# An index table moved into a loop, and three steps of the routing moved in a table of order (attention and mixture of experts, one core)

## The chip, the core and the metric

The kernel runs on one core of a Trainium2 chip. The core has a matrix engine (PE, with its weight loads PEld), a vector engine (DVE), a scalar engine (ACT), a general engine (POOL), a queue engine for transfers (SP) and 16 DMA engines. The metric is the time of one execution on the device, in microseconds (us). Before the change it was 745.78, 746.29 and 747.35 us in three runs, median 746.29.

## The reference

It computes attention over a window of 128 positions for 8 sequences of 576 tokens and 8 heads of 64, and sends every token of its output (x, 512 values) through one of 8 experts:

```python
logits = np.einsum('bsd,de->bse', x, w_gate)
local_gate = 1.0 / (1.0 + np.exp(-np.einsum('bsd,de->bse', x, w_local).squeeze(-1)))
for b in range(B):
    prev_e = -1
    for s in range(S):
        fresh_e = int(np.argmax(logits[b, s]))
        e = fresh_e if s == 0 or local_gate[b, s] < 0.5 else prev_e
        prev_e = e
        p = softmax(logits[b, s])
        h = np.maximum(x[b, s] @ w1[e], 0.0)
        out[b, s] = p[e] * (h @ w2[e])
```

The choice of a token can thus hang on that of the token before it. (The branch for prev_e below 0 is left out here; the first token is always fresh.)

## The kernel before, in words

**Attention.** The 8 batches (sequences) have 4 pairs of heads each, so there are 32 pairs. A slot of the program is one row of the table `ORDER` (lines 58 to 63, the row is the slot modulo 4), a string of atoms. Each atom names a step, and one slot holds steps of neighbouring pairs: a mark ' belongs to one pair earlier. Of a pair, `S` i computes scores (PE, tile sc), `D` adds the bias and takes the maximum (DVE), `E` the exponent (ACT), `N` divides by the sums (POOL scales nine parts in place, after a reciprocal on DVE), `U` j transposes four parts on PE (tile pt, two PSUM buffers; four matmuls, here called a turn), `C` j copies pt out (pts; ACT, but DVE for j = 0), `M` j multiplies with the values (PE, tiles xa and xb), `X` copies the weighted values out (ACT, tile xT), `T` transposes them on DVE for their storage. On each engine the instructions of this stage run in the order in which they are written down: `InOrder` (line 151) ties each to the one before it.

**Routing of a batch.** After a batch's last pair, a generator `side` is made of `tokens` (line 568) and `route` (line 589). A dot in `ORDER` advances it by one step, so the dots set where its steps stand among the attention's. The steps of `tokens`: logits of 512 tokens (PE into tile pk, lines 575 and after); the first copy of pk (ACT, to tile part); logits of the last 128; the second copy; transposes of part; a reduction on DVE to L; the same for the last tokens. Of `route`: DVE finds the freshest choice (rcb); four small matmuls bring the choices into a row (PE, pk from rcb); ACT makes a hold copy of it; DVE scans the row (hr); PE spreads it; DVE makes the one-hot oh_all; PE then counts the rank of each token within its expert (six matmuls, the first with weights utri); and more steps to the tables of own tiles. Tile pk has one PSUM buffer (line 82), so each use waits until the one before it is read. Seven batches are routed within the attention; the eighth's routing lies in the stage that follows.

**Experts.** Tokens that go to one expert are gathered in tiles of 128 rows. Each expert has a fixed number of own tiles (`OWN`, 9 in all); the rest is cut by size rank after a plan (`RANKS`, 32 tiles); and what goes beyond this plan is done in a loop at the end (line 1191), whose count `left` is read from the routing's result. A visit of the plan (`Fixed.run`) multiplies in three passes for each product (lines 953 to 955; h is the hidden layer, y the output), and at fixed places calls `Feed.tick`, which advances the generator `routing()`: the eighth batch's steps, then `rank_tables` (line 865). That one makes three tables: of ranks (`trk`), of counts, and of the tiles beyond the plan (`tfx`). A table is filled by `fill_table` (line 843): per batch, five compares on DVE (tile cw), five matmuls on PE (pk, from cw and ro_all, line 860), three additions on DVE; `indices` (line 696) turns it into addresses on DVE. In this stage instructions are written in the order of visits and ticks, with the matmuls pinned to it. The chunks of weights are loaded by SP's queue up to six ahead (wraw) and split into two parts by ACT and DVE (cut).

The scatters of results (`out<-y,sidx`) and all gathers (`kr<-xd,xidx`, `gs<-gd,ridx`) are issued by POOL.

Of the kernel before, what the change touches and what calls it, by code (L numbers as in the profile page):

```python
# [28 lines left out]
NSB = 128  # L29
# [19 lines left out]
def windows(nb):  # L49
    return [min(4 * t, nb - 4) for t in range((nb + 3) // 4)]  # L50
# [7 lines left out]
ORDER = [  # L58
# [4 lines left out]
]  # L63
DEPTH = 3
POOL_CUT = 19
# [6 lines left out]
def moe_attention(ctx, tc, qT, kT_d, vv, wg, wl, w1, w2, out):  # L72
    nc = tc.nc
# [44 lines left out]
    tfx = st.tile([P, NSB], F32, name="tfx")  # L118

    XO = 4 * KS, 4 * KS + NSB, 4 * KS + 2 * NSB  # L120
    TO = KS, KS + NTL, KS + NTL + NFX
# [4 lines left out]
    idxs = [xidx, ridx, sidx]  # L126
# [10 lines left out]
    def run(g):  # L137
        for _ in g:
            pass
# [163 lines left out]
    with ExitStack() as actx:  # L303
# [97 lines left out]
        def setup():  # L401

            yield from make_bias(2)
            yield from make_bias(3)
            whole = dict(channel_multiplier=0, allow_small_or_imprecise_dtypes=True)
            pool.memset(w32, 0.0)
            nc.sync.dma_start(w32[:, :, 0:8], wg.rearrange("(k p) e -> p k e", p=P))
            nc.sync.dma_start(w32[:, :, 8:9], wl.rearrange("(k p) e -> p k e", p=P))
            yield
            pool.memset(onesb, 1.0)  # L410
            yield
            pool.memset(msel, 1.0)
            yield
            pool.affine_select(utri, onesb, [[1, P]], ALU.is_gt, 0.0, base=0, channel_multiplier=-1)
            yield
            pool.affine_select(msel, msel, [[-32, 4]], ALU.is_ge, 0.0, base=0, channel_multiplier=1)
            yield
            pool.memset(first, 0.0)
            yield
            pool.iota(quart, [[32, 4]], base=0, **whole)  # L420
            yield
            pool.affine_select(msel, msel, [[32, 4]], ALU.is_ge, 0.0, base=31, channel_multiplier=-1)
            yield
            pool.memset(first[0:1, 0:1], 1.0)
            yield
            pool.iota(k8, [[0, NT], [-1, NE]], base=NE, **whole)
            yield
            pool.tensor_tensor(quart, quart, msel, ALU.mult)
            yield
            pool.tensor_copy(identb, ident)  # L430
            yield
            for t in HR:
                pool.memset(t, 0.0)
                yield
            pool.memset(ohs, 0.0)
            pool.memset(g32, 0.0)
            yield
            pool.iota(io16, [[0, NT], [1, 4 * KS]], base=0, **whole)
            yield
            pool.iota(rep32, [[0, 4], [1, 32]], base=0, **whole)  # L440
            yield
            pool.iota(val, [[P, NT]], base=1, channel_multiplier=1, allow_small_or_imprecise_dtypes=True)
            yield
            pool.memset(tbl, 0.0)
            yield
            pool.memset(tfx, 0.0)
            yield
            pool.memset(trk, 0.0)
            yield
            pool.memset(own, 0.0)  # L450
            for e, k in enumerate(OWN):
                pool.memset(own[:, e:e + 1], 4.0 * k)
            yield
            for r in range(NE):
                pool.memset(slots[:, 0, r:r + 1], float(sum(CAP[:r])))
                pool.memset(slots[:, 1, r:r + 1], float(CAP[r]))
                if r % 2:
                    yield
            pool.iota(io32, [[1, NFX]], base=0, **whole)
            yield  # L460
            pool.iota(io128, [[1, NSB]], base=1, **whole)
# [234 lines left out]
        def indices(t, idx, x0, c0, wins):  # L696

            xi, rw, sc = idx
            m, n = t.shape[1], len(wins)
            ti = tp.tile([P, NSB], I32, name="ti", bufs=1)[:, :m]  # L700
            bi = tp.tile([P, NSB], I32, name="bi", bufs=1)[:, :m]
            fi = tp.tile([P, 4 * NFX], F32, name="fi", bufs=1)
            dve.tensor_scalar(ti, t, -1.0, 0.0, ALU.add, ALU.max)
            dve.tensor_scalar(bi, ti, 5, None, ALU.arith_shift_right)
            yield
            dve.scalar_tensor_tensor(fi[:, :m], bi, 96.0, ti, ALU.mult, ALU.add)
            yield
            dve.tensor_scalar(xi[:, x0:x0 + m], fi[:, :m], roff[:, 0:1], None, ALU.add)
            yield
            t1 = tp.tile([P, NFX], F32, name="t1", bufs=1)[:, :n]  # L710
            z = tp.tile([P, NFX], F32, name="iz", bufs=1)[:, :n]
            fw = fi[:, :4 * n].rearrange("p (c q) -> p c q", q=4)
            lo = 0
            while lo < n:
                hi = lo + 1
                while hi < n and wins[hi] == wins[hi - 1] + 4:
                    hi += 1
                dve.tensor_tensor(fw[:, lo:hi], t[:, wins[lo]:wins[lo] + 4 * (hi - lo)].rearrange("p (c q) -> p c q", q=4),
                                  msel.unsqueeze(1).broadcast_to([P, hi - lo, 4]), ALU.mult)
                lo = hi  # L720
            dve.tensor_reduce(t1, fw, AX.X, ALU.add)
            yield
            dve.tensor_scalar(rw[:, c0:c0 + n], t1, -1.0, 0.0, ALU.add, ALU.max)
            dve.tensor_scalar(z, t1, 0.0, 16384.0, ALU.is_equal, ALU.mult)
            dve.scalar_tensor_tensor(sc[:, c0:c0 + n], t1, -1.0, z, ALU.add, ALU.add)
            yield
# [108 lines left out]
    def per_token(x, name):  # L835

        t8 = mp.tile([P, NA, NE], F32, name="ge", bufs=1)
        nc.vector.tensor_tensor(t8, oha, x.unsqueeze(1).broadcast_to([P, NA, NE]), ALU.mult)
        o = tp.tile([P, NA], F32, name=name, bufs=1)
        nc.vector.tensor_reduce(o, t8, AX.X, ALU.add)  # L840
        return o

    def fill_table(table, fc, pace):

        fo = {}

        def hot(b):
            fo[b] = tp.tile([P, NT, NSB], F16, name="cw")
            for t in range(NT):
                nc.vector.tensor_scalar(fo[b][:, t], io128, fc[:, b * NT + t:b * NT + t + 1], None, ALU.is_equal)  # L850

        hot(0)
        for b in range(NB):
            for _ in range(pace // 2):
                yield
            if b + 1 < NB:
                hot(b + 1)
            pt = ptk.tile([P, NSB], F32, name="pk")
            for t in range(NT):
                pin(nc.tensor.matmul(pt, ro_all[:, b, t], fo[b][:, t], start=t == 0, stop=t == NT - 1))  # L860
            for _ in range(pace - pace // 2):
                yield
            enter(table, pt, b)

    def rank_tables():
# [58 lines left out]
        off = small("off")  # L924
# [7 lines left out]
        nc.vector.tensor_reduce(ef, ge, AX.X, ALU.add)  # L932
        nc.vector.tensor_scalar(efx[:, 0:NFX], ef, float(NE - 1), None, ALU.min)
        yield
        b_t = per_token(off, "at_t")
        nc.vector.tensor_tensor(b_t, b_t, ka, ALU.add)
        nc.vector.scalar_tensor_tensor(b_t, b_t, 1.0, hi_t, ALU.add, ALU.mult)
        yield
        yield from fill_table(tfx, b_t, 4)
        yield from indices(tfx, idxs, XO[1], TO[1], windows(NSB))  # L940
        nc.sync.dma_start(xidx_d, xidx[:, XO[1]:])
        nc.sync.dma_start(ridx_d, ridx[:, TO[1]:])
        nc.sync.dma_start(sidx_d, sidx[:, TO[1]:])
# [153 lines left out]

    route_done, rank_done, table_done = [], [], []  # L1100

    def routing():
        yield from chain(tokens(NB - 1, last_xT), route(NB - 1))
# [85 lines left out]
    left = nc.values_load(efx[0:1, NFX:NFX + 1], min_val=0, max_val=NFX)  # L1189
    line.clear()  # L1190
    with tc.For_i(0, left, 1) as i:
        gc = mp.tile([P, 4], I32, name="gc")
        rc = mp.tile([P, 1], I32, name="rc")
        sc = mp.tile([P, 1], I32, name="sc")
        ec = mp.tile([1, 1], I32, name="ec")
        nc.sync.dma_start(gc, xidx_d.rearrange("p (c q) -> p c q", q=4)[:, bass.ds(i, 1)].rearrange("p o q -> p (o q)"))
        nc.sync.dma_start(rc, ridx_d[:, bass.ds(i, 1)])
        nc.sync.dma_start(sc, sidx_d[:, bass.ds(i, 1)])
        nc.sync.dma_start(ec, efx_d[0:1, bass.ds(i, 1)])
        ev = nc.sync.value_load(ec[0:1, 0:1], min_val=0, max_val=NE - 1)  # L1200
        v = Flex(gc, rc, sc)
        at_once(v)
        v.run(Stream([(ev, w, c) for w, c in FLEX_ORDER]), lambda: None)
        scatter(*pending.pop())
# [36 lines left out]
```

## Time and profile before

| what | us |
|---|---|
| median of three runs | 746.29 |
| the profiled execution | 746.64 |
| its span, from the first instruction to the last | 744.9 |
| PE busy | 715.9 (96%) |
| DVE busy | 504.8 (68%) |
| ACT busy | 431.4 (58%) |
| POOL busy | 403.1 (54%) |

The rows of the profile read: start, duration, engine, line, operation, the written tile, an arrow, the read tiles, the shapes; xN is a count of like instructions in a row, and [a <-b] says that the engine was idle for a us before and that b ended it. Matmuls overlap, so the distance of two starts tells what one costs. Times are us from the start of the span. In the attention stage most lines stand as L157, a helper's line; the tiles tell them apart.

### The profile page before, as it was taken

To read this page: it belongs to the slowest core of one execution; us is meant where nothing else is said; L and a number is where in the kernel's file an instruction comes from. 1 tells how busy PE (TensorE), PEld (TensorE's weight loads), DVE (VectorE), ACT (ScalarE), POOL (GpSimd) and SP (SyncE) were. 2 spreads that over 40 slices of the span, in tenths; PEclk is the share of its full clock that TensorE was granted. 3 is DMA by queue.
4 is the path that set the end of the run, shared out by engine and by line. 5 is a ranking of instruction groups with operands and counts; after the bars stand their busy time and mean duration, and the time that the engine had idled before them with its cause. 6 is when DMAs were issued, how large, how long until landed. Compare 5 with 4: busy or idle time off the path is not lost. (4 is left out here: it accounts for less than half of the span.)

```text
span 744.9 us, 15003 instructions
## 1 busy us (share of the span) xinstructions
PE 715.9 (96%) x4669; PEld 599.7 (81%) x4669; DVE 504.8 (68%) x1743; ACT 431.4 (58%) x1204; POOL 403.1 (54%) x672
## 2 busy tenths in 40 slices
PE   7999999999999998998999999999999999999996
PEld 4777777777777777886888888989989987888895
DVE  7658686776869789998667375567567556536562
ACT  7778878878877875433333254355455446434553
POOL 7664554544558586587777153744745746402121
PEclk9999999999999999999999999999999999999999
DMA  9975636555370357545455256557657656535560
GB/s 222 194 205 127 181 98 177 181 146 167 98 260 28 104 168 250 163 142 150 131 150 178 91 174 207 181 176 224 192 170 229 196 166 210 170 91 185 164 177 30
DMA packets 94724, 122.01 MB, mean 164 GB/s; under 512 B 46961, under 2 KB 65777, under 8 KB 94642
## 3 DMA queue, kind: packets, MB, share of 16 engines
q1 hardware_dynamic: 83810, 100.36, 45.2%
q0 software_dynamic: 9488, 20.22, 9.0%
q8 instruction: 37, 0.61, 0.3%
q10 hardware_dynamic: 1344, 0.46, 0.3%
q14 instruction: 45, 0.37, 0.2%
HBM read 101.29 MB, written 20.30 MB: 163 GB/s over the span
## 5 line engine op out<-in xcount | busy, mean ns | idle before, releaser
L234 DVE TENSOR_TENSOR cut<-wraw,cut 128x512 fp32r<-128x512 f32 x231 | 150.5, 687 | 51.3 <-ACT cut L232 50.1
L172 POOL DMA_INDIRECT kr<-xd,xidx x141 | 154.5, 1096 | 52.8 <-issue 40.3
L232 ACT CAST cut<-wraw 128x512 fp32r<-128x512 f32 x212 | 120.7, 618 | 56.0 <-PE y L955 55.7
L953 PE MATMUL h<-qx,cut 128*128 128x384 f32 (+6 forms) x440 | 142.7, 325 | 2.9 <-ACT qx L181 2.9
L954 PE MATMUL h<-qx,cut 128*128 128x384 f32 (+6 forms) x440 | 142.6, 324 | 0.5 <-DVE qx L182 0.5
L955 PE MATMUL h<-qx,cut 128*128 128x384 f32 (+6 forms) x440 | 142.1, 323 | 0.0
L157 POOL TENSOR_SCALAR cut<-cut,r 128x192 f32<-128x192 f32 (+2 forms) x256 | 99.6, 407 | 69.3 <-PE pt L157 41.0
L953 PE MATMUL y<-cut,hh 128*128 128x512 f32 x328 | 129.2, 394 | 1.1 <-ACT hh L998 1.1
L955 PE MATMUL y<-cut,hl 128*128 128x512 f32 x328 | 128.8, 396 | 0.5 <-DVE hl L999 0.5
L954 PE MATMUL y<-cut,hh 128*128 128x512 f32 x328 | 129.1, 393 | 0.0
L947 POOL DMA_INDIRECT out<-y,sidx x41 | 43.2, 1053 | 155.6 <-ACT y L962 120.5
L998 ACT ACTIVATE hh<-h 128x384 fp32r<-128x384 f32 (+6 forms) x104 | 47.9, 460 | 131.3 <-PE h L955 131.1
L157 PE MATMUL sc<-kr,qx 128*128 128x192 f32 (+1 forms) x576 | 110.4, 320 | 2.8 <-DVE mn L157 1.7
L157 ACT ACTIVATE cut<-scs,mn 128x192 f32<-128x192 f32 (+2 forms) x256 | 109.6, 430 | 5.5 <-DVE mn L157 3.7
L157 DVE CUSTOM_DVE_ANT_0 scs<-sc,bias 128x192 f32<-128x192 f32 (+2 forms) x288 | 86.4, 325 | 36.1 <-PE sc L157 34.1
L999 DVE SCALAR_TENSOR_TENSOR hl<-h,hh 128x384 fp32r<-128x384 f32 (+6 forms) x112 | 56.6, 505 | 71.3 <-ACT hh L998 69.4
L953 PEld LDWEIGHTS h<-qx,cut 128*128 128x128 f32 x440 | 84.0, 191 | 10.0 <-ACT qx L181 3.3
L157 PEld LDWEIGHTS sc<-kr,qx 128*128 128x128 f32 x576 | 85.5, 191 | 7.6 <-DVE mn L157 5.9
L954 PEld LDWEIGHTS h<-qx,cut 128*128 128x128 f32 x440 | 84.1, 191 | 7.1 <-DVE qx L182 0.9
L955 PEld LDWEIGHTS h<-qx,cut 128*128 128x128 f32 x440 | 84.1, 191 | 3.3 <-issue 0.2
L157 PE MATMUL pt<-ident,cut 128*128 128x128 f32 x448 | 70.3, 282 | 3.3 <-POOL cut L157 1.8
L955 PEld LDWEIGHTS y<-cut,hl 128*128 128x128 f32 x328 | 61.4, 188 | 15.0 <-DVE hl L999 2.1
(227 smaller groups left out, 1065.2 us busy)
## 6 DMA issues: line engine op xcount, KB each, us to landing
wraw<-w SPq DMA_DIRECT2D x120, 512.0 KB
xd<-T SPq DMA_DIRECT2D x8, 1152.0 KB
kr<-kT SPq DMA_DIRECT2D x31, 288.0 KB
qx<-qT SPq DMA_DIRECT2D x61, 144.0 KB
cut<-v SPq DMA_DIRECT2D x8, 1024.0 KB
kr<-xd,xidx POOLq DMA_INDIRECT x141, 4.0
v<-v SPq DMA_DIRECT2D x8, 128.0 KB
out<-y,sidx POOLq DMA_INDIRECT x41, 3.3
```

The lines of the kernel that those rows point to most:

```text
L157: ins = getattr(self.engine, name)(*args, **kw)
L172: queued(nc.gpsimd.indirect_dma_start(out=r, out_offset=None, in_=src[0:n, :], in_offset=bass.IndirectOffsetOnAxis(ap=col, axis=0), bounds ...
L232: scalar.copy(c[:, 0, f], raw[:, f])
L234: (pool if 2 * n + f == POOL_CUT else vector).tensor_tensor(c[:, 1, f], raw[:, f], c[:, 0, f], ALU.subtract)
L947: queued(nc.gpsimd.indirect_dma_start(out=out[:, :], out_offset=bass.IndirectOffsetOnAxis(ap=col, axis=0), in_=y, in_offset=None, bounds_c ...
L953: nc.tensor.matmul(o, ah, bh, start=start, stop=False)
L954: nc.tensor.matmul(o, ah, bl, start=False, stop=False)
L955: nc.tensor.matmul(o, al, bh, start=False, stop=stop)
L998: now.act.activation(hh, hp, AF.Relu)
L999: nc.vector.scalar_tensor_tensor(hl, hp, 0.0, hh, ALU.max, ALU.subtract)
```

## The change

It has two parts. First, the table of the tiles beyond the plan (tfx) is no longer filled among the experts' visits. Its first operand (b_t, 40 values for each partition) is still computed there and kept in a tile of its own; clearing, filling, indices and the stores of the three index arrays and of the experts' row stand at the start of the loop's body and are done in each turn of the loop. POOL's memset of tfx in the set-up goes. Second, dots of two rows of `ORDER` move; their number in each row stays. What the second part moves, engine by engine, for one batch (seven batches have the same):

ACT, third row of `ORDER`, around the copy of the weighted values (xT<-xa) and the copies of logits (part<-pk):

```order
-L157 ACTIVATE cut,sm<-scs,mn 128x128
-L157 ACTIVATE cut,sm<-scs,mn 128x192
-L157 COPY xT<-xa 128x384
 L157 COPY part<-pk 128x512
-L157 ACTIVATE cut,sm<-scs,mn 128x192
+L157 ACTIVATE cut,sm<-scs,mn 128x128
+L157 ACTIVATE cut,sm<-scs,mn 128x192
+L157 COPY xT<-xa 128x384
 L157 COPY part<-pk 128x128
+L157 ACTIVATE cut,sm<-scs,mn 128x192
 L157 COPY pts<-pt 128x512
```

The first copy of logits now stands ahead of two exponents and of the copy of xa; the second copy stands ahead of the exponent that it used to follow.

PE, start of the fourth row, around the four matmuls of the choices' row (pk<-identb,rcb) and the turn U0 (pt<-ident,cut):

```order
 L157 MATMUL sc<-kr,qx 128x192
+L157 MATMUL pt<-ident,cut 128x128 x4
 L157 LDWEIGHTS rcb
 L157 MATMUL pk<-identb,rcb 1x128
...
-L157 MATMUL pt<-ident,cut 128x128 x4
 L157 MATMUL sc<-kr,qx 128x192 x3
```

U0 ran behind the row's four matmuls and now runs ahead of them.

PE, end of the fourth row, around the rank's six matmuls (from utri to ohs,onesb) and the turns U2 and, of the next slot, U3:

```order
 L157 MATMUL sc<-kr,qx 128x192 x2
+L157 MATMUL pt<-ident,cut 128x128 x4
 L157 LDWEIGHTS utri
 L157 MATMUL pk<-oh_all,utri 128x40
...
 L157 MATMUL pk<-ohs,onesb 128x40
-L157 MATMUL pt<-ident,cut 128x128 x6
+L157 MATMUL pt<-ident,cut 128x128 x2
 L157 MATMUL pt<-ident,pb_140 128x128 x2
```

U2 ran behind the rank and now runs ahead of it; U3 stays behind it. On DVE the order of the attention stage is the same as before.

```diff
@@ ORDER, third and fourth row @@
-    "U3' S0 S1 S2 . E7' C2' D0 D1 U0 E8' D2 E0 N8' S3 S4 C3' S5 M0' M1' M2' M3' M4' D3 E1 E2 C0 X0' D4 . . D5 E3 . U1 C1 S6 . D6 . E4 S7 S8 . D7 E5 D8 N3 U2 E6 . X1'",
-    "U3' S0 S1 . . S2 E7' C2' . D0 D1 U0 E8' D2 E0 N8' S3 . S4 C3' S5 . M0' M1' M2' M3' M4' D3 . E1 E2 . C0 X0' D4 . D5 E3 U1 C1 T0'' S6 . D6 E4 S7 S8 D7 . E5 D8 N3 T1'' . U2 E6 X1' T0' T1'",
+    "U3' S0 S1 S2 . E7' C2' D0 D1 U0 E8' D2 E0 N8' S3 S4 C3' S5 . M0' M1' M2' M3' M4' . D3 E1 E2 C0 X0' D4 . D5 E3 U1 C1 S6 . D6 . E4 S7 S8 . D7 E5 D8 N3 U2 E6 . X1'",
+    "U3' S0 S1 . . S2 E7' C2' D0 D1 U0 . E8' D2 E0 N8' S3 . S4 C3' S5 . M0' M1' M2' M3' M4' D3 . E1 E2 . C0 X0' D4 . D5 E3 U1 C1 T0'' S6 . D6 E4 S7 S8 D7 . E5 D8 N3 T1'' U2 . E6 X1' T0' T1'",
@@ setup() @@
             pool.memset(tbl, 0.0)
-            yield
-            pool.memset(tfx, 0.0)
             yield
@@ rank_tables() @@
-        b_t = per_token(off, "at_t")
+        b_t = per_token(off, "bt")
         nc.vector.tensor_tensor(b_t, b_t, ka, ALU.add)
         nc.vector.scalar_tensor_tensor(b_t, b_t, 1.0, hi_t, ALU.add, ALU.mult)
         yield
-        yield from fill_table(tfx, b_t, 4)
-        yield from indices(tfx, idxs, XO[1], TO[1], windows(NSB))
+        beyond.append(b_t)
+
+    def beyond_table():
+        nc.vector.memset(tfx, 0.0)
+        run(fill_table(tfx, beyond[0], 0))
+        run(indices(tfx, idxs, XO[1], TO[1], windows(NSB)))
         nc.sync.dma_start(xidx_d, xidx[:, XO[1]:])
         nc.sync.dma_start(ridx_d, ridx[:, TO[1]:])
         nc.sync.dma_start(sidx_d, sidx[:, TO[1]:])
@@ the loop @@
     with tc.For_i(0, left, 1) as i:
+        beyond_table()
         gc = mp.tile([P, 4], I32, name="gc")
```

More of the change, by code (lines that the diff above doesn't have):

```diff
@@ L1096, in moe_attention @@
             visits.append(Flex(xidx[:, x:x + 4], ridx[:, c:c + 1], sidx[:, c:c + 1]) if nb == 4 else Fixed(Rows(x, c, nb, idxs)))
-    route_done, rank_done, table_done = [], [], []
+    route_done, rank_done, table_done, beyond = [], [], [], []
     def routing():
```

## The prediction

> **What bounds the kernel now.** I read the page's shares first, where PE leads, then a table of stretches (busy us of PE, its weight loads, DVE, ACT and POOL, then the granted clock, DMA's share and GB/s), then the list of waits in two stretches, one of the experts' stage and one of the attention.
>
> ```profile
> 96.00:134.00 38.00, 36.78 (x321) 29.20 (x319) 29.18 (x167) 31.21 (x119) 19.23 (x55) 1.00 0.55 157
> ...
> 400.00:500.00 100.00, 100.00 (x517) 87.56 (x515) 54.94 (x99) 43.58 (x82) 50.07 (x47) 1.00 0.52 166
> ...
> PE y L953 <- ACT hh L998: 1.1, 1, 1.1
> ...
> PE y L955 <- DVE hl L999: 0.5, 1, 0.5
> ```
>
> The two stages differ. In 400:500 PE is busy 100.00 of 100.00 us, and the waits of 400:700 hold two of its own, 1.1 and 0.5 us: there the end moves with every instruction that PE issues. DMA's share is 0.52, so a PE that is some us ahead does not run into the weights' loads. In the attention stage (96:134) PE is idle 1.2 us of 38, and the waits of 60:248 name who holds it (us in total, times, longest):
>
> ```profile
> PE pk L157 <- ACT part L157: 1.5, 5, 0.3
> PE pk L157 <- DVE oh_all L157: 1.5, 6, 0.2
> ...
> PE pk L157 <- DVE rcb L157: 1.1, 5, 0.2
> ```
>
> Each stands once in a batch. They are the three places that the table of order touches. Whether PE's stop is also the path is another question, since ACT has 31.21 busy us in the same 38.
>
> **The change part by part.** *The table of the tiles beyond.* Of L860's 80 matmuls, 40 stand in 364 to 405, eight groups of five, one per batch. The timeline of PE around the first group:
>
> ```profile
> L860 PE MATMUL pk<-cw,ro_all x40: 219/219/230, 364.1 to 405.1; 128*128 128x128 f16 x40
> ...
> 363.61 0.39 PE L954 MATMUL h<-qx,cut 128*128 128x512 f32 x1
> 363.84 0.39 PE L955 MATMUL h<-qx,cut 128*128 128x512 f32 x1
> 364.07 0.45 PE L860 MATMUL pk<-cw,ro_all 128*128 128x128 f16 x5
> 364.33 0.48 PE L953 MATMUL h<-qx,cut 128*128 128x512 f32 x1
> ...
> 365.11 0.39 PE L953 MATMUL h<-qx,cut 128*128 128x512 f32 x1
> ```
>
> The durations overlap, so the starts count. Undisturbed, one start follows the other by 0.23 us (363.61, 363.84). From 363.84 to the start of the fourth h matmul after it, 365.11 (two rows between them left out), it is 1.27 us instead of 4 x 0.227 = 0.91: a group costs 0.36 us, with the slower start of the two matmuls behind it. Eight groups are 2.9 us, all in a stretch where PE is full, so they come off the end. The DVE work that goes too (40 compares, 24 additions and the indices) lies beside PE and is worth nothing by itself; the three stores of indices leave SP's queue, where they stood between loads of weights that PE never waited for. In the loop the table costs nothing as long as the loop does not run:
>
> ```profile
> L947 POOL DMA_INDIRECT out<-y,sidx x41 | 43.2, 1053 | 155.6 <-ACT y L962 120.5
> ```
>
> 41 scatters are the 9 tiles of the own visits and the 32 of the ranks' plan; there is none from the loop.
>
> *The logits' first copy.* A batch of the middle, first PE, then ACT:
>
> ```profile
> 118.02 0.39 PE L157 MATMUL xb<-pt,v 128*64 128x128 f32 x4
> 118.71 0.43 PE L157 MATMUL pk<-xT,w 128*32 128x128 f32 x8 [0.30 <-ACT part L157]
> ...
> 126.67 0.39 PE L157 MATMUL xb<-pt,v 128*64 128x128 f32 x4
> 126.99 0.19 PE L157 MATMUL pk<-identb,rcb 128*1 128x64 f16 x1
> ...
> 117.69 0.48 ACT L157 COPY xT<-xa 128x384 f32<-128x384 f32 x1 [1.27 <-PE xa L157]
> 118.06 0.59 ACT L157 COPY part<-pk 128x512 f32<-128x512 f32 x1
> ...
> 119.20 0.27 ACT L157 COPY part<-pk 128x128 f32<-128x128 f32 x1
> 119.76 0.59 ACT L157 COPY pts<-pt 128x512 f32<-128x512 f32 x1 [0.29 <-PE pt L157]
> 120.24 0.46 ACT L157 ACTIVATE cut<-scs,mn 128x192 f32<-128x192 f32 x1
> ...
> 120.69 0.44 ACT L157 ACTIVATE cut<-scs,mn 128x192 f32<-128x192 f32 x1
> ```
>
> Where nothing waits, xb's last four matmuls take 0.32 us to the next start (126.67 to 126.99); here they take 0.69, so the stop is 0.37. The second logits' matmuls need the one pk buffer, which the copy at 118.06 empties only after ACT's copy of xa, itself late by PE. Now that copy stands in the 1.27 us in which ACT waits for PE anyway, 0.59 us that fit. The matmuls start at 118.34 and end at 118.77. But the second copy now comes ahead of an exponent: it ends at about 119.05, the exponent takes a place of 0.45 (120.24 to 120.69), and the copy of pts starts at about 119.5 instead of 119.76. ACT gains 0.3, PE 0.37; since ACT runs without a pause from pts on, I take 0.3 per batch. Seven batches go through this (the eighth's routing lies in the experts' stage): 2.1 us. From both sides: nothing, if ACT is the path there, and 7 x 0.37 = 2.6.
>
> *The choices' row and the rank behind a turn.*
>
> ```profile
> 112.92 0.94 PE L157 MATMUL sc<-kr,qx 128*128 128x128 f32 x6
> 113.78 1.06 PE L157 MATMUL pk<-xT,w 128*32 128x512 f32 x8
> ...
> 121.96 0.94 PE L157 MATMUL sc<-kr,qx 128*128 128x128 f32 x6
> 123.11 0.38 PE L157 MATMUL pk<-identb,rcb 128*1 128x128 f16 x4 [0.22 <-DVE rcb L157]
> 123.43 0.66 PE L157 MATMUL pt<-ident,cut 128*128 128x128 f32 x4
> ...
> 126.34 0.50 PE L157 MATMUL xb<-pt,cut 128*64 128x192 f32 x4
> ...
> 121.91 1.47 POOL L157 TENSOR_SCALAR cut<-cut,r 128x64 f32<-128x64 f32 x4 [2.46 <-PE pt L157]
> ...
> 124.16 0.56 ACT L157 COPY pt<-pt 128x512 f32<-128x512 f32 x1
> ...
> 128.23 0.92 PE L157 MATMUL sc<-kr,qx 128*128 128x192 f32 x4
> 129.39 0.19 PE L157 MATMUL pk<-oh_all,utri 128*128 128x40 f16 x1 [0.25 <-DVE oh_all L157]
> ...
> 131.44 0.42 PEld L157 LDWEIGHTS pt<-ident,cut 128*128 128x128 f32 x4 [0.33 <-POOL cut L157]
> ...
> 130.76 0.56 ACT L157 COPY pts<-pt 128x512 f32<-128x512 f32 x1
> ```
>
> The row: six sc matmuls take 0.86 us to the next start where nothing waits (112.92 to 113.78) and 1.15 here, a stop of 0.29. The turn (U0, four transposes) put into it needs POOL's scaled parts, and the fourth ends at 121.91 + 1.47 = 123.38, while the row's DVE result is there at 123.1. So U0's last transpose starts near 123.4 either way, and the row's four matmuls (0.32 us, 123.11 to 123.43), which filled that wait, now follow it. What is won at the head is lost behind: I take 0. The bounds: 7 x 0.29 = 2.0 gained, 7 x 0.32 = 2.2 lost. Queued behind the row are ACT's hold copy and, after it, the copy of pt at 124.16 to 124.72, which PE asks for at 126.34, 1.6 us later, and DVE's scan.
>
> The rank: from 128.23 it is 1.16 us to utri for four sc matmuls, where six issue in 0.86: a stop of 0.3 at least, and at four sixths of 0.86, 0.6 at most, into which U2's four transposes fit. But the next U0, at 131.44, comes 0.12 us after ACT's copy of pts ends (130.76 + 0.56 = 131.32), which frees its buffer, and ACT is full ahead of it:
>
> ```profile
> 127.30:131.30 4.00, 3.75 (x35) 3.02 (x34) 3.80 (x22) 4.00 (x17) 1.63 (x5) 1.00 0.26 72
> ```
>
> ACT is busy 4.00 of 4.00 us, so PE arrives earlier and waits longer. I take 0, and 7 x 0.6 = 4.2 as the far bound; a loss I exclude up to a switch of some 0.05 us, as the rank itself starts no later than DVE's oh_all lets it.
>
> **The sum.** The profiled execution took 746.64 us around a span of 744.9, 0.35 above the median of 746.29. 746.64 - 2.9 - 2.1 = 741.6; against the median 741.3.
>
> **The rivals.** *The turns pay too* (chance 0.17): if neither POOL's scaling nor ACT's copy ends last, up to 2.0 + 4.2 = 6.2 us more go; half of that gives 738.2. Against it speak the ends 123.38 and 131.32. *Only the table* (0.19): ACT and DVE set the attention's pace and PE's earlier issue turns into longer waits elsewhere: 743.4. For it speaks ACT's 31.21 of 38. *Another count of half-clock stretches* (0.06):
>
> ```profile
> 340.00:350.00 10.00, 8.17 (x28) 6.34 (x29) 7.64 (x29) 2.44 (x5) 7.87 (x8) 0.83 0.54 157
> ```
>
> In 340:350 the granted clock is 0.83, a stretch of some 3.4 us at half (0.17 x 10 / 0.5), so 1.7 us of PE's work are lost. If the earlier arrival splits a pause otherwise, one falls away: 739.7; or one is added: 742.9. [...]
>
> *Slower* (0.04): the turn ahead of the row holds PE in order. If POOL's scaling came so late that the row, its hold copy and DVE's scan start over 1.6 us later, the copy of pt reaches PE too late. To beat the 5.0 us won, each of seven batches must lose over 0.7, so POOL must end 2.3 us after 123.38; at 1.0 us a batch it is 748.3. POOL idles 2.46 us ahead of that scaling, so I see no cause for it. *The change does not do what it says* (0.04): the loop's body is longer, and the way past it may cost.
>
> ```profile
> q8 instruction: 37, 0.61, 0.3%
> ```
>
> A load of instructions took about 0.003 x 744.9 x 16 / 37 = 1 us on its engine. One or two at the exit give 742.3 to 743.3; with the 2.9 given back at later waits too, 746. [...]
>
> **How the numbers follow.** The forecast, 741.3, holds 0.50, with 740.2 to 742.8 as its own range. A difference under 0.2%, 1.5 us, cannot be told from no change. Faster by more is all of the forecast, the turns, the clock and nearly all of "only the table": 0.91. Within it 0.05, slower 0.04. The range, 738.0 to 744.0, takes in the table alone and half of the turns' gain; outside lie the turns in full, the slower case and the change that misses.
>
> **What would show it.** The tables' matmuls are 40 in all, none of them after 340 us, and the stretch behind is 2.9 us shorter. In a batch, part's wait on PE is gone, and the second logits' matmuls of two batches, 32.2 us apart now, come at 31.9:
>
> ```profile
> 150.90 0.42 PE L157 MATMUL pk<-xT,w 128*32 128x128 f32 x8 [0.30 <-ACT part L157]
> ```
>
> That is 150.90 less 118.71. At 31.4 or less the turns paid; at 32.2 ACT was the path. U0's loads at the batch's last turn should show a longer wait. A loop that runs, or pauses in 350:700 that were not there, make it wrong.

## The result and the profile after

The changed kernel took 741.86 us in the median of six runs (740.40 to 742.23), the kernel before 746.82 us in six (744.73 to 748.81): the ratio is 0.9936, with a 95% interval of 0.9918 to 0.9953. In a second series, in which both ran again, it was 742.21 us in nine runs against 746.49 in twenty, ratio 0.9935 (0.9914 to 0.9955). The change makes the kernel faster by 4 to 5 us, 0.65%. (Times here are medians of all executions; a ratio and its interval are of the fast ones alone, those within 1.5% of their kernel's fastest, so that it need not be the quotient of the two times beside it.) The profiled execution of the changed kernel took 742.23 us around a span of 740.5.

The page of the changed kernel, engine by engine: PE lost 2.7 busy us (715.9 before), DVE 13.7 (504.8 before).

```profile
PE 713.2 (96%) x4629; PEld 599.9 (81%) x4629; DVE 491.1 (66%) x1670; ACT 431.6 (58%) x1204; POOL 399.8 (54%) x671
```

**The table.** The line that fills tables holds 40 matmuls now, all of the ranks' table; its number in the changed file is L858, and the last starts at 329.9 us. The loop does not run: nothing of it stands in the trace.

```profile
L858 PE MATMUL pk<-cw,ro_all x40: 217/219/231, 312.0 to 329.9; 128*128 128x128 f16 x40
```

**The waits of the attention stage** (60 to 248 us of the changed kernel; us in total, times, longest). The three waits of PE's tile pk that the prediction quoted (on part 1.5 us, on oh_all 1.5, on rcb 1.1) are gone: PE's own list is down to two lines, and the longer one is new: a turn's matmuls wait for POOL, six times, up to half a us.

```profile
PE pt L157 <- POOL cut L157: 2.9, 6, 0.5
PE sc L157 <- DVE mn L157: 0.6, 3, 0.3
```

This is the turn U0 of the slot behind the rank, once in each batch, and not the turn that was put ahead of the choices' row. Here are the six sc matmuls behind the rank and this turn, two rows of the kernel before and then two of the changed one:

```profile
130.47 0.94 PE L157 MATMUL sc<-kr,qx 128*128 128x128 f32 x6
131.47 0.63 PE L157 MATMUL pt<-ident,cut 128*128 128x128 f32 x4
...
130.67 0.94 PE L157 MATMUL sc<-kr,qx 128*128 128x128 f32 x6
132.09 0.63 PE L157 MATMUL pt<-ident,cut 128*128 128x128 f32 x4 [0.48 <-POOL cut L157]
```

The turns' weight loads, in the list of all engines, wait for POOL 13.2 us where it was 8.7 (in e7 below, without the step of the choices' row, it is 11.2):

```profile
PEld pt L157 <- POOL cut L157: 13.2, 23, 0.8
```

**ACT in a batch of the middle** (changed kernel; the batch's first logits' matmuls start at 114.60, those of before at 113.78). The first copy of logits stands ahead, the wait for PE behind it is 0.79 us where it was 1.27, and the copy of pts starts 5.65 us after the batch's first matmul. Before it was 119.76 - 113.78 = 5.98: ACT gained 0.33.

```profile
116.30 0.59 ACT L157 COPY part<-pk 128x512 f32<-128x512 f32 x1
...
118.51 0.48 ACT L157 COPY xT<-xa 128x384 f32<-128x384 f32 x1 [0.79 <-PE xa L157]
119.64 0.27 ACT L157 COPY part<-pk 128x128 f32<-128x128 f32 x1 [0.66 <-PE pk L157]
...
120.25 0.58 ACT L157 COPY pts<-pt 128x512 f32<-128x512 f32 x1
```

**Where the time went.** Five rows of PE's timeline serve as marks in each kernel: the first logits' matmuls of the first batch routed and of the seventh, the ends of PE's two long pauses in the experts' stage, and the last matmul. First the kernel before, then the changed one.

```profile
49.42 1.07 PE L157 MATMUL pk<-xT,w 128*32 128x512 f32 x8
...
243.81 1.06 PE L157 MATMUL pk<-xT,w 128*32 128x512 f32 x8
...
293.73 0.18 PE L157 MATMUL pk<-cw,ro_all 128*128 128x48 f16 x1 [2.06 <-POOL cw L157]
...
341.38 0.73 PE L953 MATMUL h<-qx,cut 128*128 128x512 f32 x2 [2.92 <-ACT qx L181]
...
737.41 0.39 PE L955 MATMUL y<-cut,hl 128*128 128x512 f32 x1
```

```profile
50.59 1.07 PE L157 MATMUL pk<-xT,w 128*32 128x512 f32 x8
...
244.02 1.07 PE L157 MATMUL pk<-xT,w 128*32 128x512 f32 x8
...
293.89 0.18 PE L157 MATMUL pk<-cw,ro_all 128*128 128x48 f16 x1 [1.95 <-POOL cw L157]
...
340.09 0.73 PE L956 MATMUL h<-qx,cut 128*128 128x512 f32 x2 [2.90 <-ACT qx L181]
...
732.90 0.39 PE L958 MATMUL y<-cut,hl 128*128 128x512 f32 x1
```

| stretch between marks (us) | before | after | difference |
|---|---|---|---|
| start to first batch routed | 49.42 | 50.59 | +1.17 |
| six batches | 194.39 | 193.43 | -0.96 |
| to the end of the first pause | 49.92 | 49.87 | -0.05 |
| to the end of the second pause | 47.65 | 46.20 | -1.45 |
| to the last matmul | 396.03 | 392.81 | -3.22 |
| to the end of the span | 7.5 | 7.6 | +0.1 |

The last line of gain is the table's. Six batches of the attention gave 1.0 us, where the prediction's 0.3 a batch makes 1.8; the seventh lies in the stretch up to the first pause, which hardly changed. And two lines are not in the prediction's sum: a start that is 1.2 us later, and 1.45 us less between the two pauses, where nothing was moved. The experiments take the moved steps and the stretch between the pauses apart; the start is taken up behind them.

### The profile page after: what moved, and what is told of

It reads as the page before. It is cut to its first block, busy times and chain, and to the rows that moved or that the text cites. A ratio compares the mean times of both kernels' runs of the same rounds, so it can differ in the third digit from the quotient of the medians.

```text
span 740.5 us, 14838 instructions
## 1 busy us (share of the span) xinstructions
PE 713.2 (96%) x4629; PEld 599.9 (81%) x4629; DVE 491.1 (66%) x1670; ACT 431.6 (58%) x1204; POOL 399.8 (54%) x671
## 5 line engine op out<-in xcount | busy, mean ns | idle before, releaser
L234 DVE TENSOR_TENSOR cut<-wraw,cut 128x512 fp32r<-128x512 f32 x231 | 152.3, 695 | 53.5 <-ACT cut L232 52.2
L157 PE MATMUL sc<-kr,qx 128*128 128x192 f32 (+1 forms) x576 | 112.6, 326 | 2.4 <-DVE mn L157 1.7
L157 PEld LDWEIGHTS sc<-kr,qx 128*128 128x128 f32 x576 | 87.4, 195 | 7.7 <-DVE mn L157 4.7
L157 PE MATMUL pt<-ident,cut 128*128 128x128 f32 x448 | 72.0, 282 | 6.7 <-POOL cut L157 4.7
```

Source lines behind the costliest of these rows:

```text
L157: ins = getattr(self.engine, name)(*args, **kw)
L234: (pool if 2 * n + f == POOL_CUT else vector).tensor_tensor(c[:, 1, f], raw[:, f], c[:, 0, f], ALU.subtract)
```

## The experiments

The edits are small, so the diffs are given against the kernel before or the changed kernel, in the two rows of `ORDER`: the third row holds the logits' copies, the fourth the choices' row and the rank. Each series ran on a chip of its own by the record: e1 to e4 on chip 0, e5 to e8 on chip 9, e9 and e10 on chip 4, e11 and e12 on chip 2. On chips 0, 4 and 2 every kernel, the one before too, took 809 to 842 us, with long pauses in the experts' stage; there the totals say little, and I read the attention stage, which ran as on chip 9.

### e1 and e5: the table alone

The changed kernel with both rows of `ORDER` put back:

```diff
-    "... S5 . M0' M1' M2' M3' M4' . D3 E1 E2 C0 X0' D4 . D5 E3 U1 C1 S6 ..."
-    "... S2 E7' C2' D0 D1 U0 . E8' ... T1'' U2 . E6 ..."
+    "... S5 M0' M1' M2' M3' M4' D3 E1 E2 C0 X0' D4 . . D5 E3 . U1 C1 S6 ..."
+    "... S2 E7' C2' . D0 D1 U0 E8' ... T1'' . U2 E6 ..."
```

> The table goes into the loop, all rows of ORDER as before. My theory (the table's matmuls lay on a full PE): the stretch from PE's pause at about 341 us to the last y is 2.9 to 3.2 us shorter than before's 274.5 us; the distance of the second logits' matmuls from one batch to the next stays at 32.2 us; total 2.9 us less than before, up to 4.5 if the half-clock stretch at 294 us is not there. Rival (the gain behind 341 us came from the earlier arrival of the experts' stage, by the new order): the stretch stays as long and the total with it.

> The table in the loop alone once more, on another run of the chip, for the total beside the kernel before. By the first run of this kernel the attention stage does not move (194.41 us over six batches, 194.39 before), so the total should be 2.9 to 3.2 us below the kernel before (the table's share in the stretch behind 341 us). Rival (the table's absence lets something else wait): less than 2 us.

e1 took 820.98 us against 830.98 (ratio 0.9894, 0.9840 to 0.9947). Its six batches last 243.23 - 48.81 = 194.42 us, as before:

```profile
48.81 1.06 PE L157 MATMUL pk<-xT,w 128*32 128x512 f32 x8
...
243.23 1.06 PE L157 MATMUL pk<-xT,w 128*32 128x512 f32 x8
```

The stretch behind the second pause, which was to show the table's share, is among those with long pauses here and cannot be read.

e5, the same kernel beside a kernel before of 746.49 us, took 744.25 (ratio 0.9975, 0.9953 to 0.9997). In its trace the marks of the stage behind the second pause are

```profile
339.73 0.73 PE L956 MATMUL h<-qx,cut 128*128 128x512 f32 x2 [2.92 <-ACT qx L181]
...
732.65 0.39 PE L958 MATMUL y<-cut,hl 128*128 128x512 f32 x1
```

392.92 us from one to the other, against 396.03 before: 3.1 us less with the old order, as in the changed kernel. So the gain behind 341 us is the table's and not one of phase. The total's gain, 2.2 us in the median, is below the expected 2.9 to 3.2, though its interval (0.2 to 3.5 us) holds them. One piece that is missing is small: from the last matmul to the end of the span it is 7.6 to 7.95 us in the four undisturbed traces with the table in the loop (the changed kernel, e5, e6, e7), and 7.5 in both with the table among the visits (the kernel before, e8).

### e2: the order alone

The kernel before with both rows of `ORDER` from the change, the table where it was.

> The three moves in ORDER, the table where it was. My theory: batches 32.0 us apart as in the changed kernel, the stretch behind 341 us as before (274.5 us), total 1.2 us less than before, up to 2.6 if the half-clock stretch at 294 us is not there. Rival (a batch is shorter because POOL's memset and the table's work left other queues): batches 32.2 us, no gain.

It took 831.27 us against 830.98 (ratio 1.0019, 0.9976 to 1.0062), which tells nothing of 1 us. Its six batches:

```profile
48.80 1.06 PE L157 MATMUL pk<-xT,w 128*32 128x512 f32 x8
...
242.22 1.06 PE L157 MATMUL pk<-xT,w 128*32 128x512 f32 x8
```

193.42 us, 1.0 less than with the old order, just as in the changed kernel (193.43). The attention's gain comes from the order alone; neither the table nor POOL's memset has a part in it.

### e3 and e4: the order without its other steps

e3 is the changed kernel with the fourth row as before, so that of the order the logits' copy alone is moved. e4 (repeated as e7) keeps the rank behind turn U2 too and puts back only the choices' row:

```diff
-    "U3' S0 S1 . . S2 E7' C2' D0 D1 U0 . E8' ... T1'' U2 . E6 X1' T0' T1'"
+    "U3' S0 S1 . . S2 E7' C2' . D0 D1 U0 E8' ... T1'' U2 . E6 X1' T0' T1'"
```

> Table in the loop and the first copy of logits ahead (third row new), the fourth row as before. My theory (the turn ahead of the choices' row costs more than it saves): batches 31.83 to 31.9 us apart, 0.1 to 0.17 less than the changed kernel's 32.00, and 0.7 to 1.2 us less than it in total. Rival A (turns are free, the copy alone brings less than I read): 32.0. Rival B (the turns pay): 32.05 to 32.2.

> Table in the loop, the copy of logits ahead, the rank's matmuls behind turn U2, but the choices' row ahead of turn U0 as before. My theory (the rank's place is worth nothing, the choices' row behind the turn costs 0.1 to 0.17 a batch): as with the copy alone, 31.83 to 31.9 us from batch to batch. Rival A (the rank's place costs the lost part, the row is free): 32.0. Rival B (the rank's place pays and the choices' row costs all the more): 31.7 or less.

e3 took 817.47 us and e4 817.06 against 830.98 (ratios 0.9821, 0.9762 to 0.9881; 0.9841, 0.9793 to 0.9888). Six batches of e3, then of e4:

```profile
49.29 1.06 PE L157 MATMUL pk<-xT,w 128*32 128x512 f32 x8
...
241.61 1.07 PE L157 MATMUL pk<-xT,w 128*32 128x512 f32 x8
```

```profile
49.23 1.07 PE L157 MATMUL pk<-xT,w 128*32 128x512 f32 x8
...
241.56 1.07 PE L157 MATMUL pk<-xT,w 128*32 128x512 f32 x8
```

192.32 and 192.33 us. The copy alone is worth 194.42 - 192.32 = 2.10 us in six batches, 0.35 in each (I had put 0.3). The rank's place is worth nothing: it is 0.01 us over six batches. The rows behind the rank, shown above, say where its gain goes. From the four sc matmuls ahead of the rank (128.23 before, 128.85 in the changed kernel) to the six behind it, it is 2.24 us before and 1.82 in the changed kernel, 0.42 less; from these to the start of the next U0 it is 1.00 before and 1.42, 0.42 more. And the changed kernel, at 193.43, gives 1.1 of the 2.1 back: with the other two steps known, that is the choices' row behind the turn, 0.185 us a batch. Both rivals that spoke for a free or a paying row fall. (The expected 31.83 to 31.9 us holds, to 0.01 us, for the early batches: in e3 the first two stand 81.11 - 49.29 = 31.82 us apart. The later ones of the six are longer in every kernel, so that the mean of e3 is 32.05; of the kernel before it is 32.40 with 32.18 for the first.)

### e8: the choices' row behind the turn, alone

> The kernel before with one dot moved: the choices' row behind turn U0. Theory (U0's last transpose waits for POOL's fourth scaling, and the row, which covered that wait, follows it; the switch to the row's f16 matmuls and back is then in the open): 0.15 to 0.2 us more a batch, 195.3 to 195.6 us over six batches against 194.39. Rival (it costs only behind the earlier logits' copy, where POOL is later against PE): 194.4, no change. My first costing: nothing.

```diff
-    "... S2 E7' C2' . D0 D1 U0 E8' ..."
+    "... S2 E7' C2' D0 D1 U0 . E8' ..."
```

```profile
48.82 1.06 PE L157 MATMUL pk<-xT,w 128*32 128x512 f32 x8
...
244.36 0.64 PE L157 MATMUL pk<-xT,w 128*32 128x512 f32 x4
```

195.54 us over six batches, 1.15 more than before, 0.19 a batch: the same loss as behind the earlier copy. One execution took 747.20 us. So the step is a loss by itself too, and not only together with the other two.

### e6 and e7: the changed kernel, and the same without this step, side by side

> The changed kernel itself, beside the others on the same chip: 4.1 us below the kernel before (2.9 to 3.2 for the table and 7 x 0.16 = 1.1 for the order, by the run of the order alone), 193.4 us over six batches. Rival (the order brings more in the total than in the batches, as the experts' stage starts in another phase): 5 us or more.

> The changed kernel with the choices' row ahead of turn U0 again, now for its total beside the changed kernel. Theory (the turn ahead costs 0.185 a batch): 192.3 us over six batches, 7 x 0.185 = 1.3 us below the changed kernel, 5.4 below the kernel before. Rival (what the batches win is lost again at the pause before the experts' stage, where PE waits for transfers): no difference from the changed kernel, though the batches are shorter.

e6 took 742.21 us (ratio to the kernel before 0.9935, 0.9914 to 0.9955), e7 741.54 (0.9928, 0.9903 to 0.9953). The six batches of e6 are 193.41 us. Those of e7:

```profile
51.12 0.64 PE L157 MATMUL pk<-xT,w 128*32 128x512 f32 x4
...
243.38 1.06 PE L157 MATMUL pk<-xT,w 128*32 128x512 f32 x8
```

192.26: the batches are shorter by 1.15 as in e4, and by the whole way from the first batch to the end of the first pause e7 gains 1.6 us on e6 (241.69 against 243.28). Yet of these only 0.7 shows in the medians, less than the comparison can tell. The clock takes a part of the difference, as the next section shows: the granted clock of e7 is 0.991 to 0.993 in all six executions, that of e6 0.994 or 0.995 in seven of nine. So the step's loss is shown in the traces, and a faster kernel is not.

How the row's step loses is seen in PE's and POOL's timelines, at the same place of the same batch. The changed kernel, PE and then POOL:

```profile
122.40 0.94 PE L157 MATMUL sc<-kr,qx 128*128 128x128 f32 x6
123.46 0.73 PE L157 MATMUL pt<-ident,cut 128*128 128x128 f32 x4
124.13 0.38 PE L157 MATMUL pk<-identb,rcb 128*1 128x128 f16 x4
124.44 1.24 PE L157 MATMUL sc<-kr,qx 128*128 128x192 f32 x6
125.62 0.65 PE L157 MATMUL xa<-pts,cut 128*64 128x256 f32 x4
...
122.35 1.47 POOL L157 TENSOR_SCALAR cut<-cut,r 128x64 f32<-128x64 f32 x4 [1.65 <-PE pt L157]
```

e7, the row ahead of the turn:

```profile
122.53 0.94 PE L157 MATMUL sc<-kr,qx 128*128 128x128 f32 x6
123.68 0.38 PE L157 MATMUL pk<-identb,rcb 128*1 128x128 f16 x4 [0.21 <-DVE rcb L157]
123.99 0.66 PE L157 MATMUL pt<-ident,cut 128*128 128x128 f32 x4
124.48 1.14 PE L157 MATMUL sc<-kr,qx 128*128 128x192 f32 x6
125.55 0.65 PE L157 MATMUL xa<-pts,cut 128*64 128x256 f32 x4
...
122.48 1.47 POOL L157 TENSOR_SCALAR cut<-cut,r 128x64 f32<-128x64 f32 x4 [1.65 <-PE pt L157]
```

In e7 POOL's fourth scaling ends at 122.48 + 1.47 = 123.95 and the turn starts at 123.99: it waits for nothing and takes 0.49 us to the next start. In the changed kernel the turn starts at 123.46, POOL ends at 122.35 + 1.47 = 123.82, and from the turn's start to the row's it is 0.67: 0.18 more. The six sc matmuls behind the f16 row take 1.18 to the next start, those behind the turn 1.07: 0.11 more. What is saved is 0.09: from the sc matmuls ahead of the pair to its start it is 1.06 in the changed kernel and 1.15 in e7. 0.18 + 0.11 - 0.09 = 0.20, against 0.19 measured over the batches.

### The stretch between the two pauses

Between the pauses it is 47.65 us in the kernel before, 46.20 in the changed one, 46.25 in e5, 46.31 in e6, and 47.74 in e7, 47.65 in e8. These are two groups 1.4 us apart, and they do not go by the change: e7 has the table in the loop and the better order, and is in the slower group. What divides them is PE's clock behind the first pause. Here are the windows of 3.41 us on the grid on which each trace's clock changes (that of the kernel before falls to half at 294.45, 342.23 and 741.59 us, 14 and 117 windows of 3.413 us apart): us, busy time of PE, its loads, DVE, ACT and POOL, the granted clock, DMA share, GB/s. The kernel before, e7, the changed kernel, and e6:

```profile
291.04:294.45 3.41, 1.35 (x6) 0.93 (x7) 3.41 (x11) 0.87 (x2) 2.03 (x2) 1.00 0.42 134
294.45:297.87 3.42, 3.42 (x17) 3.03 (x15) 2.16 (x8) 1.72 (x4) 0.00 (x0) 0.50 0.53 171
```

```profile
290.12:293.53 3.41, 1.46 (x7) 1.03 (x7) 3.41 (x5) 0.98 (x2) 2.62 (x3) 1.00 0.10 15
293.53:296.94 3.41, 3.41 (x17) 3.02 (x15) 2.17 (x8) 1.69 (x4) 0.00 (x0) 0.50 0.83 242
```

```profile
289.56:292.97 3.41, 2.38 (x16) 1.86 (x15) 3.36 (x13) 1.93 (x4) 2.95 (x3) 1.00 0.06 16
292.97:296.38 3.41, 2.49 (x18) 2.24 (x18) 3.41 (x7) 0.06 (x1) 0.87 (x2) 1.00 0.54 156
```

```profile
291.38:294.80 3.42, 2.13 (x16) 1.92 (x15) 3.42 (x6) 0.00 (x0) 1.23 (x2) 1.00 0.40 131
294.80:298.21 3.41, 3.00 (x19) 2.39 (x18) 3.35 (x12) 3.11 (x7) 0.00 (x0) 1.00 0.56 177
...
608.83:612.24 3.41, 1.80 (x7) 1.16 (x7) 2.69 (x7) 2.56 (x6) 2.80 (x3) 1.00 0.33 113
612.24:615.65 3.41, 3.41 (x15) 3.22 (x14) 2.19 (x5) 1.65 (x4) 2.53 (x3) 0.50 0.59 161
```

The pause is the same in all, 1.95 to 2.06 us. Where it lies within one window, PE is busy 1.35 or 1.46 us of 3.41, and the next window runs at 0.50. Where it is cut by a border of the grid, PE is busy 2.38 or 2.13 us, and the clock stays at 1.00. In e6 a later pause, 1.12 us long in the first trace of this kernel, falls so that its window holds 1.80 busy us, and the next one is halved; e8 has the same pause in a window with 1.93, and the clock stays. The second pause, of 2.9 us, brought a halved window in all six traces (behind a window with 0.73 us of PE in the kernel before, 0.67 in the changed one). So in the experts' stage of these traces a stretch at half clock followed a window with 1.80 us or less of PE, and whether the first pause made such a window hung on where it fell. In the set-up this line does not hold: windows with 2.32 us (e5) and 2.15 us (e7) of PE, before 21 us, were followed by halves too, so busy time as the profile draws it does not decide it alone.

The other executions, of which only the time and the mean granted clock are on record, differ in the same way. The traces with one stretch at half clock ahead of the last matmul (the changed kernel), two (the kernel before, e5, e6, e8) and three (e7) have a mean clock of 0.995, 0.993 or 0.994, and 0.991. A mean of 0.995 stands beside 10 of the changed kernel's 15 executions, 3 of the 20 of the kernel before in the second series, 1 of e5's 12 and none of e7's 6. So the medians too compare kernels with unlike numbers of these stretches, and a part of the 4 to 5 us goes with the clock. Among the executions at 0.995 alone the changed kernel has a median of 741.3 us and the kernel before, in three, one of 744.3: 3.0 us. Why the changed kernel has the fewer stretches no run shows; e5 and e7, which each have a part of the change, do not have them.

I then tried to take the stretches away, with matmuls in both pauses whose results are overwritten (`first_rank[0]` is the first visit of the ranks' plan):

```diff
-            pT = ptk.tile([P, 4 * NS * KS], F32, name="pk")
+            pT = ptk.tile([P, 512], F32, name="pk")
+            if b == NB - 1:
+                for _ in range(5):
+                    pe.matmul(pT, utri, utri.unsqueeze(1).broadcast_to([P, 4, P]), start=True, stop=True)
+            pT = pT[:, :4 * NS * KS]
...
                 hp = ph_.tile([P, N], F32, name="h")
+                if f == 0 and self is first_rank[0]:
+                    for _ in range(9):
+                        nc.tensor.matmul(hp, utri, utri.unsqueeze(1).broadcast_to([P, N // P, P]), start=True, stop=True)
```

> The changed kernel with matmuls that do no work (utri by utri, f16, 128x512) put into PE's two long pauses: five into the one that ends at 293 us (1.95 us), nine into the one that ends at 340 us (2.9 us). Their results are overwritten by the first real matmul into the same tile. Theory (a stretch at half clock follows a window of 3.4 us in which PE was idle for some 1.6 us or more, so whether the first pause makes one depends on where it falls in the windows): with 0.85 and 0.9 us of idle left no stretch follows, in the profile and in most of the runs; the one at 340 us cost about 1.5 us, the one at 293 us about 1.4 where there was one; total 1.5 to 2 us below the changed kernel's 742.2. Rival (the half clock comes from something else, such as the loads of weights beginning): the stretches stay and the total with them, or grows by the fillers' 14 x 0.22 = 3.1 us.

> The same fillers in the kernel with the choices' row ahead of turn U0. Theory (batches are 0.185 us shorter and, with the pauses filled, the clock cannot take it back): 1.3 us below the changed kernel with fillers, about 739. Rival (what the batches win is lost at the pause before 293 us, where PE waits for a chain through POOL): equal to the changed kernel with fillers, though the batches are shorter.

> The changed kernel with the two pauses filled, once more, beside a kernel before of some 746 us this time if the chip is the other one. Theory (windows of 3.4 us with 1.6 us or more of idle PE bring the half clock): no stretch behind the pauses at 293 and 340 us, 1.5 to 2 us below the changed kernel's 742.2. Rival (another cause): stretches and total stay, or grow by up to 3.1 us.

> The same fillers with the choices' row ahead of turn U0. Theory: no stretch behind either pause, 1.3 us below the changed kernel with fillers, about 739. Rival (the pause before 293 us takes back what the batches win): equal to the changed kernel with fillers.

All four ran on chips where the kernel before takes 819 to 842 us, and there they tell nothing on the clock. e9 took 830.58 us against 830.73 (ratio 1.0068, 1.0026 to 1.0111), e11, the same kernel, 829.49 against 832.94 (0.9964, 0.9921 to 1.0007): two intervals for one kernel that do not overlap show how little a total is worth there. e10 took 826.80 (0.9898, 0.9825 to 0.9971) and e12 822.56 (0.9909, 0.9870 to 0.9947). In both pairs the kernel without the row's step is the faster one, by 3.8 and 6.9 us in the medians, which agrees in sign with 1.3 and is too much to be that alone. The six batches repeat: 193.39 and 193.48 us with the step, 192.27 and 192.28 without it. Whether filled pauses save the 1.4 us is open.

## Why the prediction was right, and where it was not

- **The sum** said 741.3, and the measurement is 741.86. It is right by its terms only in part, and the closeness of the total is luck: six batches of the attention gave 1.0 where 1.8 was put, and in the profiled pair the clock gave 1.45 that was in no term, while the start took 1.2. In the medians the clock helped as well: at a like clock, 0.995, the two kernels stand 3.0 us apart (three executions of the kernel before) and not the 5.0 of the sum. That start is no cost of the change: in e6, the same kernel, the first batch is routed at 49.39 us, and in the six undisturbed traces the mark lies anywhere from 48.82 to 51.12.
- **The table**, 2.9: its stretch became 3.2 us shorter in the changed kernel and 3.1 in e5, measured against a kernel before that repeats to 0.4 us in this stretch (396.03, and 395.63 in e8). In e7 it is 392.83 us, in e6, with a stretch at half clock in it, 394.17. The reading held that a group costs its start-to-start distance, not its durations, and that PE is full there. A little comes back at the end of the program, where the span's tail is 0.1 to 0.5 us longer in the kernels with the larger loop body. That is in the direction of the prediction's case of a costly exit from the loop, at less than the 1 us it gave to one load of instructions; that a load of instructions is the cause is not shown.
- **The logits' copy**, 0.3 a batch: 0.35 by e3. The mechanism is the one given: the copy fits in ACT's wait for PE, the second logits' matmuls follow at once, and ACT reaches pts 0.33 us sooner. Whether ACT or PE sets the pace, on which the prediction chose 0.3 and not 0.37, is not shown: the distance of two early batches fell from 32.18 to 31.82 us, by 0.36, and the mean lies between ACT's 0.33 and PE's 0.37.
- **The choices' row behind the turn**, 0: the step that failed, and the one that held back half of the attention's gain. It costs 0.185 a batch, some 1.3 us over seven; up to the end of the first pause it is 1.6 between e6 and e7. The prediction's sentence was "U0's last transpose starts near 123.4 either way". It does not. In the kernel before, the turn starts at 123.43, after POOL's end at 123.38, and so runs without a wait; the row ahead of it, 0.31 us that PE had to do anyway, was what let POOL finish. Moved ahead, the turn runs into POOL's end, 0.18 us, and the row is left uncovered behind it. The gain at the head, 0.29 by the prediction's bound, is 0.09 in the trace: the turn cannot start at once either, as its parts leave POOL one by one until 123.82. The bounds (2.0 gained, 2.2 lost) held it; the value taken between them did not.
- **What the prediction had not priced** in this step is the place of the f16 matmuls: the six sc matmuls cost 0.11 us more behind the row than behind the turn. (The switch of some 0.05 us that it allowed for at the rank was its author's estimate, and no run shows it; measured are this 0.11 us and, in the kernel before, 0.31 us in place of 0.23 from the first h matmul behind a group of the table's f16 ones to the next, 364.33 to 364.64.)
- **The rank behind a turn**, 0: right in size, and in that the next U0's wait takes the gain up: PE comes 0.42 us sooner out of the rank and waits as much longer at that turn. What the wait is for was read too narrowly. The prediction named ACT's copy of pts, which ends at 131.32; but the row that it shows names POOL, whose scaling ends at 129.87 + 1.46 = 131.33. In the changed kernel they end at 131.94 and 131.95. With 0.01 us between them the traces cannot tell which holds PE.
- **The rivals.** *The turns pay too* has the wrong sign for one and nothing for the other. *Only the table* is refuted by the batches of e2. *Another count of half-clock stretches* happened, in the profiled pair, beside the forecast: the changed kernel's trace has one stretch less, worth 1.45 us, and by their clocks so have most of its executions. (By the prediction's own 1.7 us its two times would be 739.6 and 743.0.) That it can differ with no change at all is seen in e6, which is the changed kernel again, and has one more than the first trace of it, at 612 us. *Slower* had the first half of the mechanism (the turn holds PE in order, POOL comes late); a late copy of pt, by which it was to lose, was not needed, and the loss was a quarter of the 0.7 us a batch that it asked for.
- **The signs that it named**: 40 matmuls, none after 340 us, 2.9 us less behind; part's wait gone; U0's loads waiting longer. All came, with 3.2 for the 2.9; U0's loads beside the choices' row wait 0.39 us for POOL in the changed kernel, and not at all before. Batches at 31.9 was what it said for its own case, 32.2 for none; in the pair of batches that it named the distance is 32.00, between the two, and that was the first sign of a step that costs.

## What to carry to other kernels

When a piece of work is moved out of a wait, ask what it covered there: here a row of four small matmuls filled the time in which another engine finished the next one's operand, and moved behind, both stood open. A term of zero with bounds of both signs is best tested by undoing that one edit, and read from the period of a repeated stretch: here six batches repeated to 0.1 us from run to run, while totals moved by 3 us. And before a gain between two totals is put down to an edit, look at the granted clock behind each pause, since here whether a pause of 2 us cost 1.4 us more hung on where it fell.

## What the runs showed of the hardware

Half-clock stretches started on a grid of 3.41 us (14 and 117 windows apart in the kernel before), and in the experts' stage the window before each held 1.80 us (e6) or less of PE's work, while behind one of 1.93 us (e8) the clock stayed full (six traces). And six f32 matmuls took 0.11 us longer from start to start behind the row of four small f16 matmuls (1.18) than behind four f32 transposes (1.07); why is not shown.

The kernel before took 746 us on chip 9 and 831 to 833 us on chips 0, 4 and 2, in the medians. The attention stage was the same to 0.1 us in six batches; the time was lost in the experts' stage, in long pauses and at a lower clock (a mean of 0.955 in e1's trace, 0.993 in the kernel before's). Of e1, PE's waits between 260 and 440 us begin with

```profile
PE y L956 <- issue: 8.7, 2, 8.0
```

where "issue" is time in which PE waited for nothing that the profile shows; the changed kernel's undisturbed trace has no PE wait of that kind in that place. The cause was not found, and as each series ran on one chip, the record cannot tell the chip from the occasion.
